# Output projection in row-split runs behind the first layer, one sum moved from GpSimd to VectorE, and the last product cut in two

## The chip, the core and the metric

The kernel runs on one core of a Trainium2 chip. The time is device time in microseconds, the median of several executions. The record gives each execution a state, fast or slow, by its time and its granted TensorE clock (1.0 is full speed). Engines are named as the profile names them: PE is TensorE, DVE is VectorE, ACT is ScalarE, POOL is GpSimd, SP is the engine that issues transfers.

## The reference

One transformer block on x of 2048 rows and 576 columns: linear attention with 32 heads of width 18, then a feed-forward layer of width 4608. Only its second half matters here:

```python
x = x + ga * _A_ref(h, A_wqkv, A_w_phi, A_wo)      # attention, ends in "o @ wo"
h = _layernorm(x, axis=-1) * (1 + cb) + sb
x = x + gb * _B_ref(h, B_w1, B_w2)                 # relu(h @ w1) @ w2
```

## The kernel before

After a first part (weights, keys, values, queries; some 93 us) the kernel goes through eight blocks of two row tiles (256 rows). Each block has a first layer `l1` and a second layer `l2`. The second layer is done as one level of a Strassen-like scheme: seven products (`prod`) of 18 matmuls, on sums of quarter matrices, in banks X = 6, Y = 4, Z = 7 of PSUM, the memory that matmuls write. The results pass through a buffer `yt`, which has one half for each half of the output's columns. A row-split run is one in which two matmuls of 64 rows each work side by side, on the lower and the upper 64 partitions. In the gaps of block b the two tiles of block b + 1 are prepared through hooks: query sums (`q_fin`), attention numerators and their division (`num_mm`, `num_o`), a transposing transfer (`turn_dma`), the output projection (`wo_mm`), the second normalization, and the scaling of the transposed result h2 that the next first layer reads.

```python
    def wo_mm(t, pr, add_x):
        for k in range(2):
            # (add_x: first part of the kernel only)
            for ci in range(NC):                      # NC = 5 chunks of 128 rows; 576 = 4 * 128 + 64
                pe.matmul(pr[:, k, 0:HD], lhsT=oT[:, t % 2, ci, :], rhs=wo_sb[:, ci, k * HD:(k + 1) * HD],
                          start=(ci == 0 and not add_x), stop=(ci == NC - 1))

    def l1_rest(js, u, hb):                           # the row-split run: two halves of 64 rows side by side
        for n, j in enumerate(js):
            for hf in range(2):
                b0 = 64 * hf
                pe.matmul(PS[:, 2 * u + hf, n * 256:n * 256 + 256], lhsT=w1b[b0:b0 + 64, j * P:(j + 1) * P],
                          rhs=hb[b0:b0 + 64, 4, :], start=False, stop=False, skip_group_check=True)

    # l1: three groups g; in each: full chunks, l1_rest for u = 0..2, remaining full chunks and relu, hooks(g, u)
    # l2: seven prod; hooks(pos) ahead of every nine matmuls
        prod(Y, A12, B21, al, True)
        fin(t, 0, Y, 0)
        if b > 0:
            pool.tensor_tensor(out=A12, in0=A12, in1=U2, op=ALU.subtract)
    # ... A12 is read again by the last product, prod(Z, A12, B22, al)

        def in_l1(g, u):
            # ...
            if (g, u) in ((0, -1), (0, 1)):
                # q_fin(q), q_in(q + NL)
            if (g, u) in ((1, 2), (2, 1)):
                t = t0 + g - 1
                pr = pair(3)                          # banks 6 and 7
                num_mm(t, pr)
                num_o(t, pr)
                turn_dma(oT[:, t % 2], o_sb[:, t % 2, :])

        def in_l2(pos):
            # pos 1 and 4: wo_mm, residual addition, statistics; pos 2 and 6: normalization, turn_dma to h2;
            # pos 12: five tensor_scalar that scale h2
```

The softmax here doesn't subtract the row's maximum and nothing guards it: scores larger than these inputs give would overflow.

## Time and profile before

| | before |
|---|---|
| time | 392.11 us (391.75 to 392.55, the 3 runs known before the change ran) |
| span of the profiled execution | 390.7 us |
| first part, until the first matmul of block 0 | 93.5 us |
| each of blocks 0 to 6, first matmul to first matmul | 37.05 us |
| block 7, first matmul to last matmul's start | 33.63 us |
| from there to the end | 4.20 us |

### The profile page before, as it was taken

What the parts mean: (1) busy time and instruction counts of PE and PEld (TensorE: products, weight loads), DVE (VectorE), ACT (ScalarE), POOL (GpSimd) and SP (SyncE); (2) the same over time, 40 slices, a digit from 0 to 9 for tenths busy, and PEclk for the clock granted to TensorE, in tenths of its full rate; (3) what the DMA queues carried; (4) which work ended last, traced back from release to release, by engine and by line L of the source; (5) the groups of instructions that cost most, each with busy time, mean ns of one, the idle gap of its engine ahead of it and who ended that gap; (6) DMA issues with size and microseconds to landing.
All of it is one profiled execution on the core that took longest, in us unless ns stands there. A gap on an engine that the chain in (4) does not pass through costs nothing.

```text
span 390.7 us, 8908 instructions
## 1 busy us (share of the span) xinstructions
PE 383.8 (98%) x3693; PEld 311.7 (80%) x3693; DVE 244.3 (63%) x452; ACT 157.9 (40%) x360; POOL 142.3 (36%) x199
## 2 busy tenths in 40 slices
PE   8999999999999999999999999999999999999995
PEld 4778888878887888788888878887888788878874
DVE  0889998854879746573755567458555664653221
ACT  1798779699531233124213510531143123312510
POOL 2155858741101510740164045306510641072045
PEclk9999999999999999999999999999999999999999
DMA  7999739795732151125313311450143124010001
GB/s 291 418 420 403 274 133 354 178 306 161 189 65 35 47 121 20 35 61 109 35 27 83 80 35 32 107 65 19 47 93 35 24 69 51 18 34 33 3 0 32
DMA packets 49515, 44.36 MB, mean 114 GB/s; under 512 B 39361, under 2 KB 42050, under 8 KB 48706
## 3 DMA queue, kind: packets, MB, share of 16 engines
q1 hardware_dynamic: 49186, 43.59, 39.6%
q8 instruction: 29, 0.48, 0.5%
q10 hardware_dynamic: 288, 0.19, 0.2%
q14 instruction: 12, 0.10, 0.1%
HBM read 27.97 MB, written 6.49 MB: 88 GB/s over the span
## 4 chain that ended last, share of the span: by engine, by line
PE 86%; POOL 6%; ACT 2%; DVE 2%; DMA 2%; issue 1%; SPq 0%; POOLq 0%; DVEq 0%; ACTq 0%
PE PS L683 33%; PE PS L742 29%; PE PS L274 9%; PE PS L410 5%; PE PS L690 5%; POOL wo_sb L637 2%; PE PS L235 2%; PE PS L391 1%; ACT RT L279 1%; POOL RH L754 1%; DMA gatd<-gt 1%; PE PS L324 1%; POOL RT L291 1%; DMA ga_row<-gatd 1%; DVE st L240 1%
## 5 line engine op out<-in xcount | busy, mean ns | idle before, releaser
L683 PE MATMUL PS<-h,R 128*128 128x256 bf16 x1152 | 133.5, 273 | 0.0
L683 PEld LDWEIGHTS <-R 128*128 128x128 bf16 x1152 | 109.8, 98 | 17.5 <-issue 5.1
L742 PEld LDWEIGHTS <-RH 128*128 128x128 f16 x864 | 84.5, 98 | 21.8
L728 POOL TENSOR_TENSOR yt<-yt,gb_row 128x288 f32<-128x288 f32 x23 | 16.8, 731 | 167.0 <-DVE yt L727 167.0
L742 PE MATMUL PS<-R,RH 128*128 128x288 bf16 (+1 forms) x576 | 75.6, 286 | 0.0
L697 ACT ACTIVATE RH<-PS 128x256 f16<-128x256 f32 x72 | 27.7, 384 | 114.0 <-PE PS L690 107.4
L699 DVE SCALAR_TENSOR_TENSOR RH<-PS,RH 128x256 f16<-128x256 f32 x72 | 30.1, 419 | 68.2 <-ACT RH L697 68.2
L279 ACT ACTIVATE RT<-PS,rs 128x576 bf16<-128x576 f32 x64 | 43.0, 750 | 7.5 <-PE PS L274 7.1
L698 ACT ACTIVATE RH<-PS 128x512 f16<-128x512 f32 x72 | 42.9, 595 | 7.8 <-PE PS L683 6.5
L746 ACT ACTIVATE RS<-PS 128x288 f32<-128x288 f32 x24 | 9.9, 411 | 75.9 <-PE PS L742 75.9
L742 PE MATMUL PS<-RT,RH 128*128 128x288 f16 x288 | 37.9, 286 | 0.0
L274 PE MATMUL PS<-RH,R 116*128 116x288 bf16 x240 | 31.8, 286 | 0.5 <-ACT RH L631 0.5
L754 POOL TENSOR_TENSOR RH<-RH,RT 128x2304 f16<-128x2304 f16 x7 | 31.8, 4548 | 0.0
L274 PE MATMUL PS<-RH,RT 116*128 116x288 bf16 x240 | 31.7, 286 | 0.0
L274 PEld LDWEIGHTS <-R 116*128 116x128 bf16 x240 | 22.9, 98 | 6.4 <-issue 0.7
L274 PEld LDWEIGHTS <-RT 116*128 116x128 bf16 x240 | 22.7, 98 | 5.5
L420 DVE TENSOR_SCALAR xn<-x_sb,mv,rs 128x576 bf16<-128x576 bf16 (+1 forms) x28 | 22.4, 842 | 7.3 <-ACT rs L415 7.3
L729 POOL TENSOR_TENSOR x_sb<-yt,x_sb 128x288 bf16<-128x288 f32 x31 | 22.8, 737 | 5.9 <-DVE yt L725 4.1
L240 DVE BATCH_NORM_STATS2 st<-x_sb 128x6 f32<-128x288 bf16 x60 | 24.2, 445 | 0.5
L410 PE MATMUL PS<-wo_sb,oT 128*128 128x288 bf16 x160 | 22.6, 286 | 0.2 <-POOL wo_sb L637 0.2
L284 DVE TENSOR_REDUCE Rk<-RT 128x64 f32<-128x1152 bf16 x16 | 21.2, 1332 | 1.4 <-ACT RT L279 1.4
L284 DVE TENSOR_REDUCE Rq<-RT 128x64 f32<-128x1152 bf16 x16 | 21.5, 1342 | 0.0
(115 smaller groups left out, 414.2 us busy)
## 6 DMA issues: line engine op xcount, KB each, us to landing
R<-in_w1a_dram SPq DMA_DIRECT2D x4, 1152.0 KB
eqd<-RT SPq DMA_DIRECT2D x14, 288.0 KB, 5.8
RT<-eqd SPq DMA_DIRECT2D x14, 288.0 KB, 2.7
R<-in_w2a_dram SPq DMA_DIRECT2D x3, 864.0 KB, 10.4
R<-in_w2b_dram SPq DMA_DIRECT2D x2, 1296.0 KB, 10.9
out_dram<-x_sb SPq DMA_DIRECT2D x15, 144.0 KB, 3.3
RT<-in_xT_dram SPq DMA_DIRECT2D x2, 640.0 KB
x_sb<-in_xk_dram SPq DMA_DIRECT2D x3, 288.0 KB
```

The costliest lines, as they stand in the source:

```text
L240: dve.bn_stats(out=s[:, hf, :], in_=x_sb[:, t, hf * HD:(hf + 1) * HD])
L274: pe.matmul(pr[:, k, 0:HD], lhsT=xt(t, ck), rhs=w[0:R, ck, k * HD:(k + 1) * HD], start=(ck == 0), stop=(ck == NC - 1))
L279: act.activation(out=E.rearrange("p (b h s e) -> p b h s e", b=2, s=2, e=DH)[:, :, :, s, :], in_=pr[:, :, 0:HD].rearrange("p b (h e) -> p ...
L284: dve.tensor_reduce(out=Rr, in_=E.rearrange("p (c e) -> p c e", e=DH), axis=AXX, op=ALU.add)
L410: pe.matmul(pr[:, k, 0:HD], lhsT=oT[:, t % 2, ci, :], rhs=wo_sb[:, ci, k * HD:(k + 1) * HD], start=(ci == 0 and not add_x), stop=(ci == NC ...
L683: pe.matmul(PS[:, 2 * u + hf, n * 256:n * 256 + 256], lhsT=w1a[:, ci, jj * P:(jj + 1) * P], rhs=hb[:, ci, :], start=(n == 0 and ci == 0), ...
L697: act.activation(out=A11[:, j, :], in_=lo[:, :, 0, :], func=ACT.Relu)
L698: act.activation(out=A2[:, j, :, :], in_=PS[:, 2 * u + 1, :].rearrange("p (n s f) -> p n s f", n=2, s=2), func=ACT.Relu)
L699: dve.scalar_tensor_tensor(out=U3[:, j, :], in0=lo[:, :, 1, :], scalar=0.0, in1=A11[:, j, :], op0=ALU.max, op1=ALU.subtract)
L729: pool.tensor_tensor(out=x_sb[:, t, c], in0=y, in1=x_sb[:, t, c], op=ALU.add)
L742: pe.matmul(PS[:, bank, 0:HD], lhsT=am[:, j, :], rhs=bm[:, j, :], start=first and j == 0, stop=(j % 9 == 8), skip_group_check=True)
L754: pool.tensor_tensor(out=A12, in0=A12, in1=U2, op=ALU.subtract)
```

## The change

Its intent: the projection's fifth chunk has only 64 real rows, and still costs two full matmuls a tile. From block 2 on, these 64 rows lie twice (in both halves of the partitions), so that both column halves run as one row-split pair, right behind the first layer's own row-split run. For that, attention moves forward in the block, and the query sums into the block before. One 2304-wide sum goes from GpSimd to VectorE from block 2 on. The last product of the kernel is cut into two column halves.

```diff
+    def wo_rest(t, pr):
+        for k in range(2):
+            b0 = 64 * k
+            pe.matmul(pr[:, k, 0:HD], lhsT=oT[b0:b0 + 64, t % 2, 4, :], rhs=wo_sb[b0:b0 + 64, 4, k * HD:(k + 1) * HD],
+                      start=True, stop=False, skip_group_check=True)
+    # wo_full: the chunks 0 to 3, eight full matmuls
         if b > 0:
-            pool.tensor_tensor(out=A12, in0=A12, in1=U2, op=ALU.subtract)
+            (pool if b == 1 else dve).tensor_tensor(out=A12, in0=A12, in1=U2, op=ALU.subtract)
 # in l1, after the l1_rest of a group:
+            hooks(g, "rest")
 # hooks of the first layer
+            if b < 2:
+                # as before, and:
+                if b and (g, u) == (2, 2):
+                    q_next(t0 + 2)
+                return
+            if (g, u) in ((0, 0), (0, 2)):
+                attend(t0 + u // 2)
+            if g and u == "rest":
+                wo_rest(t0 + g - 1, pair(3))
+            if g and u == 0:
+                t = t0 + g - 1
+                wo_full(t, pair(3))
+                add_res(t, pair(3))
+                bn(1, t)
+            if (g, u) == (1, 2):
+                norm2(b, t0)
 # hooks of the second layer: norm2 of the second tile at pos 1, scaling of h2 at pos 8 (pos 12 if b < 2)
+            if b > 1 and pos in (4, 10) or b == 1 and pos == 8:
+                q_next(t0 + 2 + pos // 8)
 # attend: before its turn_dma
+        if t > 5:
+            act.activation(out=o_sb[:, t % 2, D:640], in_=o_sb[:, t % 2, 512:D], func=ACT.Copy)
 # tail of the last block: yl = part of the result, made ready on VectorE and GpSimd ahead of fin(t + 1, 0, X, None)
+        for i, bank in enumerate((Z, 0)):
+            c, g = slice(i * H4, (i + 1) * H4), slice(HD + i * H4, HD + (i + 1) * H4)
+            for j in al:
+                pe.matmul(PS[:, bank, c], lhsT=A12[:, j, :], rhs=B22[:, j, c], ...)
+            dve.tensor_tensor(out=yt[:, 0, c], in0=PS[:, bank, c], in1=gb_row[:, g], op=ALU.mult)
+            dve.tensor_tensor(out=x_sb[:, t, g], in0=yt[:, 0, c], in1=yl[:, c], op=ALU.add)
 # layout of the input wo
+    wo[D:] = g["A_wo"][512:]
```

(The lines with # are remarks.)

More of the change, by code (lines that the diff above doesn't have):

```diff
@@ L403, in turn_dma, with wo_mm @@
         sp.dma_start_transpose(dst, src.rearrange("p (c f) -> p c f", f=P))
-    def wo_mm(t, pr, add_x):
+    def wo_mm(t, pr, add_x=False):
         for k in range(2):
@@ L411, in wo_mm, with add_res @@
                           start=(ci == 0 and not add_x), stop=(ci == NC - 1))
+    def add_res(t, pr):
+        x = v2(x_sb[:, t, :])
+        dve.tensor_tensor(out=x, in0=x, in1=pr[:, :, 0:HD], op=ALU.add)
     def ln2_rs(t):
@@ L415, in ln2_rs, with ln2_apply @@
         act.activation(out=rs2[:, t, 0:1], in_=lnv[:, t:t + 1], func=ACT.Exp, scale=-0.5)
-    def ln2_apply(t, src):
+    def ln2_apply(t, src=None):
         def cols(o, i):
@@ L466, in tile_block @@
     SS = RS[:, 0:6 * HD].bitcast(FP32).rearrange("p (a f) -> p a f", f=HD)
+    yl = RE[:, 0:2 * HD].bitcast(FP32)
     X, Y, Z = 6, 4, 7
@@ L763, in l2 @@
         fin(t + 1, 1, Z, 2)
+        H4 = HD // 2
+        if b + 1 == NB:
+            dve.tensor_tensor(out=yl[:, H4:HD], in0=PS[:, Z, H4:HD], in1=SS[:, 1, H4:HD], op=ALU.add)
+            dve.tensor_copy(out=yl[:, 0:H4], in_=SS[:, 1, 0:H4])
+            pool.tensor_tensor(out=yl, in0=yl, in1=gb_row[:, HD:D], op=ALU.mult)
+            pool.tensor_tensor(out=yl, in0=yl, in1=x_sb[:, t, HD:D], op=ALU.add)
         prod(X, A22, T4, al)
@@ L771, in l2, with q_next, attend, wo_full @@
             return
-        rows, z = slice(t * P, (t + 1) * P), yt[:, 1, :]
+        rows = slice(t * P, (t + 1) * P)
         sp.dma_start(outf[rows, 0:HD], x_sb[:, t, 0:HD])
-        pool.tensor_tensor(out=z, in0=SS[:, 1, :], in1=gb_row[:, HD:D], op=ALU.mult)
-        pool.tensor_tensor(out=z, in0=z, in1=x_sb[:, t, HD:D], op=ALU.add)
-        prod(Z, A12, B22, al)
-        dve.tensor_tensor(out=yt[:, 0, :], in0=PS[:, Z, 0:HD], in1=gb_row[:, HD:D], op=ALU.mult)
-        dve.tensor_tensor(out=x_sb[:, t, HD:D], in0=yt[:, 0, :], in1=z, op=ALU.add)
+        for i, bank in enumerate((Z, 0)):
+            c, g = slice(i * H4, (i + 1) * H4), slice(HD + i * H4, HD + (i + 1) * H4)
+            for j in al:
+                pe.matmul(PS[:, bank, c], lhsT=A12[:, j, :], rhs=B22[:, j, c], start=(i == 1 and j == 0),
+                          stop=(j == NK - 1), skip_group_check=True)
+            dve.tensor_tensor(out=yt[:, 0, c], in0=PS[:, bank, c], in1=gb_row[:, g], op=ALU.mult)
+            dve.tensor_tensor(out=x_sb[:, t, g], in0=yt[:, 0, c], in1=yl[:, c], op=ALU.add)
         sp.dma_start(outf[rows, HD:D], x_sb[:, t, HD:D])
     NB = NT // 2
+    def q_next(q):
+        if q < NT:
+            q_fin(q)
+            if q + NL < NT:
+                q_in(q + NL)
+    def attend(t):
+        pr = pair(3)
+        num_mm(t, pr)
+        num_o(t, pr)
+        if t > 5:
+            act.activation(out=o_sb[:, t % 2, D:640], in_=o_sb[:, t % 2, 512:D], func=ACT.Copy)
+        turn_dma(oT[:, t % 2], o_sb[:, t % 2, :])
+    def wo_rest(t, pr):
[3 more added lines that the diff above has]
+                      start=True, stop=False, skip_group_check=True)
+    def wo_full(t, pr):
+        for k in range(2):
+            for ci in range(4):
+                pe.matmul(pr[:, k, 0:HD], lhsT=oT[:, t % 2, ci, :], rhs=wo_sb[:, ci, k * HD:(k + 1) * HD],
+                          start=False, stop=(ci == 3), skip_group_check=True)
+    def norm2(b, t):
+        ln2_rs(t)
+        ln2_apply(t)
+        i = t % 2
+        turn_dma(h2[:, (b + 1) % 2, :, i * P:(i + 1) * P], xn[:, i, :])
     for b in range(NB):
@@ L788, in in_l1 @@
                 return
-            if (g, u) in ((0, -1), (0, 1)):
-                q = t0 + max(u, 0)
-                q_fin(q)
-                if q + NL < NT:
-                    q_in(q + NL)
-            if (g, u) in ((1, 2), (2, 1)):
-                t = t0 + g - 1
-                pr = pair(3)
-                num_mm(t, pr)
-                num_o(t, pr)
-                turn_dma(oT[:, t % 2], o_sb[:, t % 2, :])
+            if b < 2:
+                if (g, u) in ((0, -1), (0, 1)):
+                    q_next(t0 + max(u, 0))
+                if (g, u) in ((1, 2), (2, 1)):
+                    attend(t0 + g - 1)
+                if b and (g, u) == (2, 2):
[6 more added lines that the diff above has]
+            if g and u == 0:
+                t = t0 + g - 1
+                wo_full(t, pair(3))
[3 more added lines that the diff above has]
+                norm2(b, t0)
         def in_l2(pos):
@@ L803, in in_l2 @@
                 return
-            if pos in (1, 4):
+            if b < 2 and pos in (1, 4):
                 i = pos // 4
-                t = t0 + i
-                pr = pair(i)
-                wo_mm(t, pr, False)
-                dve.tensor_tensor(out=v2(x_sb[:, t, :]), in0=v2(x_sb[:, t, :]), in1=pr[:, :, 0:HD], op=ALU.add)
-                bn(1, t)
-            if pos in (2, 6):
-                i = pos // 4
-                t = t0 + i
-                ln2_rs(t)
-                ln2_apply(t, None)
-                turn_dma(h2[:, (b + 1) % 2, :, i * P:(i + 1) * P], xn[:, t % 2, :])
-            if pos == 12:
+                wo_mm(t0 + i, pair(i))
+                add_res(t0 + i, pair(i))
+                bn(1, t0 + i)
+            if b < 2 and pos == 2:
+                norm2(b, t0)
+            if pos == (6 if b < 2 else 1):
+                norm2(b, t0 + 1)
+            if pos == (12 if b < 2 else 8):
                 hb = h2[:, (b + 1) % 2]
```

## The prediction

> **What bounds the kernel now.** I read the page first: span, busy shares, clock.
>
> ```profile
> span 390.7 us, 8908 instructions
> ...
> PE 383.8 (98%) x3693; PEld 311.7 (80%) x3693; DVE 244.3 (63%) x452; ACT 157.9 (40%) x360; POOL 142.3 (36%) x199
> ...
> PEclk9999999999999999999999999999999999999999
> ```
>
> TensorE is busy 98% of the span at the full granted clock, and no other engine passes 63%. Busy shares can hide waits, so the next view is the chain of work that ended last, in order of time, for one steady block (block 5, 278.93 to 315.98 us). Columns: start, duration, what.
>
> ```profile
> 278.93 3.06 PE PS L683 x28
> 281.99 0.76 PE PS L690 x12
> 282.75 5.35 PE PS L683 x48
> ...
> 296.32 0.38 PE PS L391 x10
> 296.69 1.31 PE PS L683 x12
> 298.00 1.20 PE PS L742 x9
> 299.20 1.23 PE PS L410 x10
> 300.43 3.31 PE PS L742 x27
> 303.73 1.23 PE PS L410 x10
> 304.96 11.03 PE PS L742 x90
> ```
>
> The whole block is TensorE and the pieces join end to end: 37.05 us, the period of all seven blocks that prepare a next one. Rates: L683 (full, 256 wide) 3.06/28 = 0.109 us each; L742 and L410 (full, 288 wide) 11.03/90 = 0.1226 us each; L690 (64 rows, 256 wide) 12 in 0.76. The output projection is the two L410 runs, 2.46 us a block. Two things are not at the plain rate. Six pairs of L690 at 0.109 would be 0.66 us, so its run costs some 0.1 us more. And the first nine L742 take 1.20 instead of 9 x 0.1226 = 1.10 us. For that I looked at the timeline around 298 us.
>
> ```profile
> 296.16 0.54 PE L391 MATMUL PS<-kvz,RE 128*128 128x76 bf16 x10
> ...
> 297.12 0.76 DVE L399 TENSOR_TENSOR o_sb<-PS,rden 128x576 bf16<-128x576 f32 x1
> ...
> 297.94 1.26 PE L742 MATMUL PS<-R,RH 128*128 128x288 bf16 x9
> ```
>
> L391 (attention numerators) writes banks 6 and 7; VectorE's L399 reads them until 297.88; 0.06 us later the first product starts, which overwrites bank 6. TensorE waited about 0.1 us for VectorE here. In the chain 1.19 or 1.20 stands at this place in each of the seven blocks; the last block, without attention, goes through at the plain rate (36 in 4.42).
>
> Last, the timeline of the tail.
>
> ```profile
> 382.51 0.46 DVE L727 TENSOR_TENSOR yt<-PS,RS 128x288 f32<-128x288 f32 x1 [6.16 <-POOL RH L754]
> 383.05 0.73 POOL L728 TENSOR_TENSOR yt<-yt,gb_row 128x288 f32<-128x288 f32 x1 [0.57 <-DVE yt L727]
> ...
> 384.42 2.37 PE L742 MATMUL PS<-R,RH 128*128 128x288 bf16 x18
> ...
> 385.98 0.33 SPq L766 DMA_DIRECT2D out_dram<-x_sb  x1
> ...
> 386.89 0.46 DVE L777 TENSOR_TENSOR yt<-PS,gb_row 128x288 f32<-128x288 f32 x1 [1.75 <-PE PS L742]
> 387.49 0.46 DVE L778 TENSOR_TENSOR x_sb<-yt 128x288 bf16<-128x288 f32 x1
> 387.98 0.33 SPq L779 DMA_DIRECT2D out_dram<-x_sb  x1
> ```
>
> The chain names GpSimd's 4.5 us sum (L754) here, but I do not read it as the bound: the product that L727 needs ended at the same moment (the next 18 start at 384.42 - 18 x 0.1226 = 382.21; their predecessor is readable about 0.3 us later). The end hangs on TensorE, two VectorE operations and one store.
>
> **What the Trainium skill says.** "TensorEngine Tiling (Array Packing)", Key Properties: changing the tiling mode drains the TensorE, while tiles of one mode work in parallel. The trace agrees: a row-split run costs 0.1 us over its six pair times. "TensorE: Matmul & The Clock Gate", Back-to-back issue gap: N/2.4 + 2.5 ns, 122.5 for N = 288 (measured 122.6) and 62.5 for N = 144 (no such full matmul here; taken as an estimate). "SBUF — State Buffer", Who interferes with whom: a VectorE operation in a two-port mode and a GpSimd operation exclude each other. It agrees: the normalization (L420) beside L754 took 2.89 us, elsewhere in the block 0.64. "VectorE: DVE Perf Modes", the errata section: an fp32 tensor_tensor takes (N+151)/0.96 ns, 457 for 288 (measured 0.46 us), so 307 for 144.
>
> **Part 1, the projection (blocks 2 to 6, ten tiles).** Ten full matmuls a tile become eight, plus two of 64 rows. The fifth chunk has only 64 real rows; their copy at partitions 64 to 127 lets both column halves run as one pair, in banks 6 and 7, directly behind the L690 run, so no mode change is added. Before: 10 x 0.1226 = 1.226. After: 8 x 0.1226 + one pair 0.123 = 1.104. Gain 0.122 a tile, 1.22 us in ten.
>
> **Part 2, the wait at the products.** Attention moves to the first group of the first layer, and the last reader of banks 6 and 7 becomes the residual addition (0.75 us) behind the third group's first part; 20 matmuls (2.2 us) follow before the product. The 0.095 us wait should go: 5 x 0.095 = 0.48 us. Blocks 0 and 1 keep the old order.
>
> **Part 3, work moved off TensorE.** L754 (4.55 us on GpSimd) becomes about 1.36 us on VectorE, the duration of the same sum in block 0. Its reader is the last product of the block, 13 us after the first or later: no gain for TensorE in itself. VectorE's second-layer stretch gains this 1.36 and two query sums (1.34 + 0.35 each), and loses two residual additions, their statistics and one normalization to the first layer. It was busy 11.9 of 18 us; there is room. ScalarE gets ten copies of 64 columns, some 0.3 us each.
>
> **Part 4, the tail.** The last product is split in two halves of 144 columns: 36 x 62.5 = 2.25 instead of 18 x 122.5 = 2.21 us, +0.04. The last two VectorE operations shrink from 0.46 to 0.31 each. Against that stands a reuse. The half products go through the same half of yt that GpSimd's addition for the next row tile still reads, and two GpSimd operations now come ahead of that addition: from 383.05 five at 0.81, 0.69, 0.81, 0.69, 0.73 end at 386.8 instead of 385.96. Only then can the first half start: 386.84, then two pairs with spacings of about 0.45 and 0.23 (scaled from 0.60 and 0.38 between the long ones), last end 388.3 instead of 387.95. The tail loses about 0.35. The store before it (144 KB, 3.3 us to landing) also starts 0.85 later and lands together with the last one, so I take +0.4.
>
> **Sum.** -1.22 - 0.48 + 0.4 = -1.3 us: 392.1 - 1.3 = 390.8.
>
> **Rivals.** (a) A wait takes the place of the one removed: the pair needs the transposed output. The numerators now start at the block's start + 3.75 and the pair is due at + 10.6. Numerators 0.38, reciprocal and product on VectorE 1.3, ScalarE's copy 0.3, transpose 2.6 to landing: ready near + 8.7, nearly 2 us early. The slowest transpose took 4.3, which still just fits. For a stall: ScalarE takes its work in order, so the copy holds back the second relu until VectorE is done. If it stalled 0.5 us in each of five blocks, the gain would be gone: about 393. (b) VectorE becomes the bound at the seam between blocks (in block 5, its scaling of h2 before 315.98 is already close). In blocks 2 to 6 that scaling comes earlier now, but block 1 has two query sums more. One late seam costs 1 us: about 392. (c) The tail gains after all, if GpSimd's addition is early enough or the stores overlap better: -0.25 instead of +0.4, so 390.1. (d) GpSimd's relief is worth more, if the chain through L754 were real: then up to 1 us in the last block, 389.8. Against it stands the coincidence at 382.5 with the product's own end.
>
> **Range and chances.** The projection's gain is counted from exact rates and nearly certain; the wait's is likely; the tail is uncertain by half a microsecond either way, and a small new wait is the main danger upward. Range 390.0 to 391.8. Two per cent is 7.8 us; the projection as a whole is 2.46 us a block, and nothing here could save or cost that much: 0.98 within, 0.01 on either side.
>
> **What would show it.** Right: the chain is still all TensorE with blocks 2 to 6 near 36.7 us and blocks 0 and 1 at 37.05; the row runs with the pair last 0.88 instead of 0.76; the full part of the projection is 8 in 0.98; the first nine products take 1.10; L420 no longer has 2.9 us cases from block 2 on; in the tail the first half operation on VectorE starts when GpSimd's last addition ends. Wrong: TensorE waits ahead of the 64-row pair or at a block's first matmuls, a block at 37 us or more, or a last store issued no later, relative to the last matmul, than before.

## The result

The changed kernel takes 390.91 us (390.52 to 391.73, 4 runs); the kernel before took 392.23 us (391.75 to 392.55, 4 runs). The ratio is 0.9969, with a 95% interval of 0.9954 to 0.9984: within 2%, and clear of 1. Ratios here and below are taken from the fast runs of the same rounds; they are not quite the ratio of the medians that are quoted.

The page of the changed kernel, first its head, engine shares and clock:

```profile
span 389.3 us, 8937 instructions
...
PE 381.7 (98%) x3711; PEld 310.7 (80%) x3711; DVE 244.6 (63%) x462; ACT 157.6 (40%) x370; POOL 119.6 (31%) x193
...
PEclk9999999999999999999999999999999999999998
```

TensorE is still the bound. GpSimd lost 22.7 us of work, VectorE's total hardly moved. The chain of work of block 5, in order of time (start, duration, what):

```profile
277.83 3.06 PE PS L688 x28
280.89 0.76 PE PS L695 x12
281.65 0.48 PE PS L391 x10
...
287.75 0.76 PE PS L695 x12
288.51 0.12 PE PS L815 x2
288.63 1.09 PE PS L821 x8
289.71 5.24 PE PS L688 x48
...
299.11 15.43 PE PS L748 x126
```

L688, L695 and L748 are the old L683, L690 and L742. The projection is L815 (the pair of 64 rows, 0.12 us) and L821 (eight full matmuls). All 126 matmuls of the seven products now go at one rate, 15.43/126 = 0.1225 us, with no slow start. The change out of the row-split mode was charged to the L683 run behind it before (5.35 us for 48); now L821 carries it (1.09 instead of 8 x 0.1225 = 0.98), and the 48 of L688 take 5.24.

Where the time went, from the start times of the matmuls:

| us | before | changed | changed, once more |
|---|---|---|---|
| first part | 93.52 | 92.83 | 92.37 |
| blocks 0 and 1, each | 37.05 | 37.05 | 37.05 |
| block 2 | 37.05 | 37.31 | 37.31 |
| blocks 3 to 6, each | 37.05 | 36.71 | 36.71 |
| block 7 to its last matmul | 33.63 | 33.74 | 33.74 |
| from there to the end | 4.20 | 4.44 | 4.45 |

So four blocks gain 0.34 us each, block 2 loses 0.26 where it should have gained 0.34, and the tail loses. (The right column is a later run of the unedited changed kernel.) The 0.6 us of block 2 are a new wait, which the timeline of the changed kernel shows at the seam of blocks 1 and 2:

```profile
157.14 4.54 POOL L760 TENSOR_TENSOR RH<-RH,RT 128x2304 f16<-128x2304 f16 x1
...
159.17 2.89 DVE L424 TENSOR_SCALAR xn<-x_sb,mv,rs 128x576 bf16<-128x576 bf16 x2 [1.21 <-ACT rs L419]
...
163.78 0.25 POOL L346 TENSOR_TENSOR ratq<-Rq,rq 128x32 f32<-128x32 f32 x1 [2.10 <-DVE rq L343]
...
165.37 2.69 DVE L872 TENSOR_SCALAR h<-h,mod 128x256 bf16<-128x256 bf16 x5
...
166.04 1.42 POOL L735 TENSOR_TENSOR x_sb<-yt,x_sb 128x288 bf16<-128x288 f32 x2
...
167.60 2.60 PE L688 MATMUL PS<-h,R 128*128 128x256 bf16 x21 [0.29 <-DVE h L872]
```

Block 2 starts at 166.93 with two matmuls, and the third waits until 167.60 for L872, VectorE's scaling of h2, whose five operations take 2.69 us instead of 1.78. They stop while GpSimd's additions (L735) run, until 167.46. The third matmul comes 0.45 us late and the fourth another 0.15. The same place before:

```profile
166.06 1.78 DVE L820 TENSOR_SCALAR h<-h,mod 128x256 bf16<-128x256 bf16 x5
166.22 0.77 POOL L729 TENSOR_TENSOR x_sb<-yt,x_sb 128x288 bf16<-128x288 f32 x1 [0.64 <-DVE yt L725]
...
167.62 1.58 PE L683 MATMUL PS<-h,R 128*128 128x256 bf16 x13
```

There only one addition of GpSimd fell beside the scaling, and it started after the scaling had. In the changed kernel, GpSimd's queue in block 1 is late. The 4.5 us sum (L760) stayed there in this block, but it stood there before too, without such a wait. New is the query sum behind it: its VectorE part follows the normalization (L424, 2.89 us beside the sum), its GpSimd part (L346) waits for that, and the additions come after it, so that three GpSimd operations instead of one now fall beside the scaling.

The tail of the changed kernel:

```profile
384.27 0.74 POOL L735 TENSOR_TENSOR x_sb<-yt,x_sb 128x288 bf16<-128x288 f32 x1
...
385.04 0.31 DVE L791 TENSOR_TENSOR yt<-PS,gb_row 128x144 f32<-128x144 f32 x1 [1.67 <-POOL x_sb L735]
...
386.28 0.33 SPq L793 DMA_DIRECT2D out_dram<-x_sb  x1
```

The first half operation L791 starts just as GpSimd's addition for the other tile ends (384.27 + 0.74 = 385.01).

### The profile page after: what moved, and what is told of

Read it like the earlier page. It is cut to its first block, busy times and chain, and to the rows that moved or that the text cites. A ratio compares the mean times of both kernels' runs of the same rounds, so it can differ in the third digit from the quotient of the medians.

```text
span 389.3 us, 8937 instructions
## 1 busy us (share of the span) xinstructions
PE 381.7 (98%) x3711; PEld 310.7 (80%) x3711; DVE 244.6 (63%) x462; ACT 157.6 (40%) x370; POOL 119.6 (31%) x193
## 4 chain that ended last, share of the span: by engine, by line
PE 87%; DVE 4%; DMA 3%; ACT 2%; POOL 2%; issue 1%; SPq 1%; POOLq 0%; DVEq 0%; ACTq 0%
PE PS L688 33%; PE PS L748 30%; PE PS L274 9%; PE PS L695 5%; PE PS L821 3%; PE PS L410 2%; PE PS L391 2%; DMA R<-in_wsc_dram 1%; ACT RT L279 1%; PE PS L324 1%; DVE RT L479 1%; DMA gatd<-gt 1%; DVE st L240 1%; DMA ga_row<-gatd 1%; PE PS L251 1%
## 5 line engine op out<-in xcount | busy, mean ns | idle before, releaser
L688 PE MATMUL PS<-h,R 128*128 128x256 bf16 x1152 | 132.8, 273 | 0.3 <-DVE h L872 0.3
L688 PEld LDWEIGHTS <-R 128*128 128x128 bf16 x1152 | 111.1, 98 | 15.5 <-issue 2.5
L748 PEld LDWEIGHTS <-RH 128*128 128x128 f16 x846 | 82.8, 98 | 20.8
L734 POOL TENSOR_TENSOR yt<-yt,gb_row 128x288 f32<-128x288 f32 x23 | 23.1, 1002 | 192.1 <-DVE yt L733 192.1
L748 PE MATMUL PS<-R,RH 128*128 128x288 bf16 (+1 forms) x558 | 72.4, 286 | 0.0
L704 DVE SCALAR_TENSOR_TENSOR RH<-PS,RH 128x256 f16<-128x256 f32 x72 | 29.0, 414 | 65.6 <-ACT RH L702 65.6
L748 PE MATMUL PS<-RT,RH 128*128 128x288 f16 x288 | 37.9, 286 | 0.0
L274 PEld LDWEIGHTS <-RT 116*128 116x128 bf16 x240 | 22.7, 98 | 5.5
L733 DVE TENSOR_TENSOR yt<-PS,RS 128x288 f32<-128x288 f32 x23 | 10.4, 453 | 26.2 <-PE PS L748 19.2
L735 POOL TENSOR_TENSOR x_sb<-yt,x_sb 128x288 bf16<-128x288 f32 x31 | 22.6, 730 | 2.4 <-DVE yt L731 0.6
L695 PE MATMUL PS<-h,R 64*128 64x256 bf16 x288 | 19.9, 271 | 0.0
L291 POOL TENSOR_TENSOR RT<-RT,ratq 128x576 bf16<-128x576 bf16 x16 | 19.0, 1190 | 1.2
```

The source lines that it names most:

```text
L274: pe.matmul(pr[:, k, 0:HD], lhsT=xt(t, ck), rhs=w[0:R, ck, k * HD:(k + 1) * HD], start=(ck == 0), stop=(ck == NC - 1))
L688: pe.matmul(PS[:, 2 * u + hf, n * 256:n * 256 + 256], lhsT=w1a[:, ci, jj * P:(jj + 1) * P], rhs=hb[:, ci, :], start=(n == 0 and ci == 0), ...
L704: dve.scalar_tensor_tensor(out=U3[:, j, :], in0=lo[:, :, 1, :], scalar=0.0, in1=A11[:, j, :], op0=ALU.max, op1=ALU.subtract)
L734: pool.tensor_tensor(out=y, in0=y, in1=gb_row[:, c], op=ALU.mult)
L735: pool.tensor_tensor(out=x_sb[:, t, c], in0=y, in1=x_sb[:, t, c], op=ALU.add)
L748: pe.matmul(PS[:, bank, 0:HD], lhsT=am[:, j, :], rhs=bm[:, j, :], start=first and j == 0, stop=(j % 9 == 8), skip_group_check=True)
```

## The experiments

All kernels gave correct results. The theory after the result: a tile gains 0.122 us by the pair and a block 0.095 us by the removed wait; the seam of block 2 loses 0.6 us to GpSimd's late work in block 1; the tail loses up to 0.35 us; the first part's 0.7 us are chance. The rival: GpSimd's relief, or the moved place, brings the gain.

**The sum on VectorE in block 1 too**

```diff
-            (pool if b == 1 else dve).tensor_tensor(out=A12, in0=A12, in1=U2, op=ALU.subtract)
+            dve.tensor_tensor(out=A12, in0=A12, in1=U2, op=ALU.subtract)
```

> The changed kernel, with the 2304-wide sum on VectorE in block 1 too. The changed kernel's trace has block 2 at 37.31 us against 36.71 for blocks 3 to 6: after its second matmul TensorE waits some 0.6 us for VectorE's scaling of h2. Theory: that scaling was late because in block 1 GpSimd holds the 4.5 us sum, and then everything behind it, beside VectorE's scaling. With the sum on VectorE, block 2 takes 36.71 us and the kernel is 0.6 us shorter than the changed one (about 390.3 us); all other blocks stay. Rival: VectorE simply has too much to do in block 1 (two query sums were added); then another 1.36 us on it leaves the wait or makes it longer, block 2 at 37.3 to 38.5 us.

Measured: 390.50 us, ratio to before 0.9960 (0.9944 to 0.9977). Block 2 takes 36.72 us, and the other blocks are as they were. Timeline of this run at the seam:

```profile
165.51 1.78 DVE L872 TENSOR_SCALAR h<-h,mod 128x256 bf16<-128x256 bf16 x5
...
167.07 3.11 PE L688 MATMUL PS<-h,R 128*128 128x256 bf16 x27
```

The scaling is back at 1.78 us, and block 2 starts with 27 matmuls in a row. VectorE had one more 1.36 us operation and was still in time, so it was not too much work but GpSimd's long sum, and the queue behind it, that made the scaling late. The normalization takes 0.64 us in this run, and the query sum's GpSimd part comes 2.2 us earlier in the block. The theory holds.

**The sum on GpSimd in all blocks**

```diff
-            (pool if b == 1 else dve).tensor_tensor(out=A12, in0=A12, in1=U2, op=ALU.subtract)
+            pool.tensor_tensor(out=A12, in0=A12, in1=U2, op=ALU.subtract)
```

> The changed kernel, with the sum on GpSimd in all blocks from 1 on, as before the change. Theory: the reader of the sum comes so much later that the engine does not matter for TensorE: blocks 3 to 6 stay at 36.71 us, block 2 at 37.3, tail within 0.1 us, whole time within 0.2 us of the changed kernel (391). Rival: GpSimd's relief is a part of the gain; then blocks 3 to 6 grow to 36.9 us or more, or TensorE waits at their first matmuls as in block 2 (37.3).

Measured: 393.64 us, ratio 1.0039 (1.0024 to 1.0054): longer than before, within 2% but clear of 1. Blocks 2 to 6 take 37.68, 37.54, 37.54, 37.08 and 36.72 us. The theory's part on the sum falls. Timeline of this run in the second layer of block 2:

```profile
195.17 6.44 DVE L872 TENSOR_SCALAR h<-h,mod 128x256 bf16<-128x256 bf16 x5
195.18 4.64 POOL L760 TENSOR_TENSOR RH<-RH,RT 128x2304 f16<-128x2304 f16 x1
...
201.53 0.45 DVE L733 TENSOR_TENSOR yt<-PS,RS 128x288 f32<-128x288 f32 x1
...
202.03 2.37 PE L748 MATMUL PS<-R,RH 128*128 128x288 bf16 x18 [0.20 <-DVE yt L733]
```

The scaling of h2, which the new order puts earlier, now falls beside GpSimd's sum and takes 6.44 us. The next VectorE operation, L733, reads bank 7, and the last product must not add to that bank before; it starts 0.37 us late (488 ns after the matmul ahead of it instead of 122). VectorE's second query sum is late too, and after it the transfers. In blocks 3 and 4 the first row-split pair then waits for its transposed input: in block 3 it starts 554 ns after the matmul ahead instead of 106. So the reader of the sum was indeed not the issue; the engine that the sum sat on was, through VectorE. The sum's move is needed for the new order, though it gains nothing by its own result.

**Ten full matmuls at the new place**

```diff
     def wo_rest(t, pr):
-        # the pair of 64 rows
+        pass
     def wo_full(t, pr):
-        # eight full matmuls
+        wo_mm(t, pr)
 # and without the copy of 64 columns in attend, so that the padding rows stay zero
```

> The changed kernel, with the ten full matmuls of before (zero rows kept) at the new place, instead of one pair of 64 rows and eight full ones. Theory: each tile costs 0.122 us more, blocks 3 to 6 go from 36.71 to 36.95 us, the whole 1.2 us longer than the changed kernel (about 392.1), and the first products still start without a wait. Rival: the gain came from the moved place and the relieved engines, not from the pair; then the blocks stay within 0.1 us of 36.71.

Measured: 392.17 us, ratio 1.0003 (0.9988 to 1.0018). Blocks 3 to 6 take 36.96 us, block 2 has 37.56 with the same wait at its start. The chain of this run in block 5 has, in place of the pair and the eight:

```profile
288.89 1.33 PE PS L410 x10
```

The pair is worth 0.25 us a block, 0.124 a tile, as expected. Without it the new order gives nothing in all: by block times its removed wait is eaten up by the waits at block 2 and in the tail.

**The removed wait alone, in the kernel before**

```diff
-            if (g, u) in ((1, 2), (2, 1)):
+            if (g, u) in ((1, 2), (2, 0)):
```

> The kernel before, with one edit: the second tile's attention numerators come one step earlier in the third group (after its first pair of products instead of its second). Theory: TensorE waits 0.095 us in each of blocks 0 to 6 for VectorE's reading of banks 6 and 7; with 0.87 us more time that wait goes and each block takes 36.96 us instead of 37.05, the whole 0.67 us less than before. Rival: the 0.095 us is a cost of changing from one product to the next and stays: 37.05.

Measured: 391.13 us, ratio 0.9979 (0.9964 to 0.9994). All seven blocks take 36.96 us. The chain of this run at the first products of block 5:

```profile
296.23 1.10 PE PS L742 x9
297.33 1.23 PE PS L410 x10
```

Nine products in 1.10 us instead of 1.20. It was a wait, and one word in the kernel before takes it away in seven blocks, where the change did so in five.

**The pair at the old place, in the kernel before**

```diff
-                wo_mm(t, pr, False)
+                if b > 1:
+                    wo_rest(t, pr)
+                    wo_full(t, pr)
+                else:
+                    wo_mm(t, pr, False)
 # with the copy of 64 columns for b > 1, and the doubled rows in the layout of wo
```

> The kernel before, with the pair of 64 rows and eight full matmuls in blocks 2 to 6, but at the old place among the second layer's products, so that each pair is a row-split run of its own. Theory: each pair saves 0.122 us but its two mode changes cost about 0.1 us each, so each tile loses some 0.07 us and blocks 2 to 6 take about 37.2 us against 37.05; the whole 0.7 us longer than before. Rival: mode changes cost little for a short run, or are hidden; then the blocks shrink to 36.8 us and the place does not matter.

Measured: 393.37 us, ratio 1.0020 (0.9994 to 1.0045). Blocks 2 to 6 take 37.23 us: 0.18 more than before. The chain of this run in block 2:

```profile
187.81 0.23 PE PS L787 x2
188.04 1.09 PE PS L793 x8
```

A pair that is a run of its own takes 0.23 us instead of 0.12, and the eight full ones behind it 1.09 instead of 0.98. That is two mode changes of 0.11 us against 0.12 us saved. The times alone leave it unclear, the blocks do not. The place behind the first layer's own run is what makes the pair pay.

**The tail of the kernel before**

The edit takes the tail's lines of the diff above back and leaves the rest.

> The changed kernel with the tail of the kernel before (one product 288 wide, two long VectorE operations, the two GpSimd operations behind the addition for the next tile). Theory: the changed tail costs 0.35 us (0.11 until the last matmul, 0.24 from it to the end); with the old one the time from the last block's start to the end of the span goes from 38.2 back to 37.8 us and the kernel is 0.35 us shorter than the changed one. Rival: the changed tail saves time by its shorter last operations; then this run's is longer.

Measured: 391.00 us, ratio 0.9961 (0.9944 to 0.9977). 33.63 us to the last matmul, and 4.18 from there to the end. In the trace the expected 0.35 us are there (some 0.27 of it are the last store, which takes more or less time from run to run, as told below); in the times, 0.9961 against 0.9969 (and 0.9967 in the repeated run) is in the right direction but inside the intervals.

**The half products through the other half of yt**, on top of the sum on VectorE in block 1

```diff
-            dve.tensor_tensor(out=yt[:, 0, c], in0=PS[:, bank, c], in1=gb_row[:, g], op=ALU.mult)
-            dve.tensor_tensor(out=x_sb[:, t, g], in0=yt[:, 0, c], in1=yl[:, c], op=ALU.add)
+            dve.tensor_tensor(out=yt[:, 1, c], in0=PS[:, bank, c], in1=gb_row[:, g], op=ALU.mult)
+            dve.tensor_tensor(out=x_sb[:, t, g], in0=yt[:, 1, c], in1=yl[:, c], op=ALU.add)
```

> The changed kernel with the sum on VectorE in block 1 as well, and the last half products going through the other half of yt, which GpSimd's late addition does not read. Theory: the half products' VectorE operations waited for GpSimd's addition; now the first starts about 1 us earlier, right after its matmuls, the last store is issued 0.35 us earlier relative to the last matmul (1.1 instead of 1.45 us), and the time from the last matmul's start to the end falls from 4.44 to about 4.1. Rival: the end is set by the store of the next row tile, which is issued 0.2 us after the last matmul's start; then the end stays at 4.4.

Measured: 390.24 us, ratio 0.9945 (0.9921 to 0.9970). The last store is issued 1.10 us after the last matmul's start instead of 1.45, and the end comes 3.88 us after it. Timeline of this run, the first half operation:

```profile
383.27 0.31 DVE L791 TENSOR_TENSOR yt<-PS,gb_row 128x144 f32<-128x144 f32 x1 [0.67 <-PE PS L789]
```

It now waits for its matmuls and no longer for GpSimd: the reuse of yt was the wait. That is the 0.35 us of the store's issue. The rest of the fall to 3.88 lies in the store itself, from its issue to the end: 2.78 us here, 2.99 in the changed kernel. In this run the cut tail is better than the old one (33.74 + 3.88 = 37.62 us against 33.63 + 4.20 = 37.83), but a store can take longer: in the run with the row-split projection from block 1 on (below), which has the same tail, it took 3.06 us and the tail 33.74 + 4.17 = 37.91.

**The sum on VectorE in block 1, and the old tail**

> The changed kernel with the sum on VectorE in block 1 as well and the tail of the kernel before. If both costs (0.6 us at block 2, 0.35 us in the tail) are real and independent, this is 0.95 us shorter than the changed kernel: about 389.9 us, 2.3 us under the kernel before. If the sum on VectorE in block 1 does not help, only the tail's 0.35 us remain.

Measured: 390.25 us, ratio 0.9944 (0.9926 to 0.9961). Block 2 takes 36.72 us, the tail 33.63 + 4.18. In the trace both costs are gone at once. The time fell by 0.7 us against the changed kernel's first measurement rather than 0.95, which the spread of whole executions covers.

**All together**: the sum on VectorE in block 1, the other half of yt, and the earlier numerators in blocks 0 and 1

> Together: the changed kernel, the sum on VectorE in block 1 too, the half products through the other half of yt, and in blocks 0 and 1 the second tile's numerators one step earlier. Expected from the single runs: blocks 0 and 1 at 36.96 us, blocks 2 to 6 at 36.71, 33.74 from the last block's start to the last matmul and 3.9 from it to the end. Against the changed kernel that is 0.18 + 0.60 + 0.3 to 0.55, some 1.1 us: about 389.8 us, ratio to the kernel before 0.993 to 0.995. If the parts interfere, a block is longer than that.

Measured: 389.55 us (389.26 to 390.27, 6 runs), ratio 0.9933 (0.9918 to 0.9949). Blocks 0 and 1 take 36.96 us, 2 to 6 36.71 or 36.72, then 33.74 and 3.88. Everything adds up, and this version beats both kernels: 2.55 us under the kernel before (392.10 in these rounds) and 1.29 under the changed one (390.84 in these rounds).

**The row-split projection from block 1 on**, on top of that. In block 0, the query sums of tiles 4 and 5 go into the first layer, and blocks from 1 on use the new order.

> As the combination of all waits, and the row-split projection at the new place from block 1 on, with the query sums for block 1's tiles in the first layer of block 0. Expected if block 0 has room on VectorE for two more query sums (3.4 us): block 1 at 36.71 us instead of 36.96, 0.25 us less than the combination. If not, TensorE waits at the first matmuls of block 1 or in block 0's products, and block 0 or 1 is longer than 37.05.

Measured: 391.62 us, ratio 0.9987 (0.9973 to 1.0001). A miss: block 0 takes 38.69 us, block 1 36.82. In block 0 TensorE waits 1.1 us at the first projection for its transposed input. In the trace SP issues the first of these transposes 18.2 us into the block instead of 15.2, behind two transfers of an added query sum (that they are what holds it up is argued, not tried). It waits once more at the last product, for VectorE. Block 0 has no room for two more query sums, which fits that the change begins with block 2.

**The changed kernel once more**

> The changed kernel, unedited, once more, for two open points. Theory: the time up to the first block (93.52 us in the trace of before, 92.83 in that of the changed kernel) varies from execution to execution and is no effect of the change; it falls somewhere between 92.1 and 93.6 again, while blocks 0 and 1 are 37.05, block 2 is 37.3 and blocks 3 to 6 are 36.71 as in the first trace. The time from the last matmul's start to the end was 4.44 us in the first trace and in one run with the same tail, 4.15 and 4.19 in two others: one of these two values again, so that 0.11 us of the tail's cost (until the last matmul) is certain and the rest is not. Time against before: ratio 0.996 to 0.998. Rival: the first part is really shorter in the changed kernel and never above 93.1.

Measured: 390.84 us, ratio 0.9967 (0.9954 to 0.9981). Block times as in the first trace, to 0.01 us (the right column of the table above). The first part took 92.37 us. Over all traces it lies between 92.19 and 93.52: three traces with the old order have 93.52, 93.27 and 92.19, ten with the new one (the changed kernel's two and eight edits of it) 92.37 to 93.12, mean 92.79. The rival for this point said never above 93.1, and with one trace at 93.12 and the lowest of all in the old order, I take no effect from it, though a few tenths can't be ruled out.

## Why the prediction was right

The number came out: 390.8 us predicted, 390.91 and 390.84 measured, in the range both times. Step by step:

- **Part 1, the pair: right.** 0.122 us a tile predicted; 0.124 by the run with ten full matmuls. One sign came out otherwise: "8 in 0.98" is 1.09 us, because the change out of the row-split mode, not added but moved, now falls on these eight.
- **Part 2, the wait: right.** 0.095 us a block predicted; the kernel before with earlier numerators shows 0.09 in each of seven blocks. Together a block gains 0.34 us, as predicted (36.7 us stood in the text).
- **Part 3, work moved off TensorE: wrong in one sentence.** The step that failed is "no gain for TensorE in itself", read from the reader of the sum alone. With the sum left on GpSimd the kernel takes 2.7 us more than the changed one (0.7 points of ratio), because the sum then holds up VectorE's earlier scaling of h2. "There is room" on VectorE held. The kernel as changed pays for this too: in block 1 the sum was left on GpSimd, and the 0.6 us wait at the start of block 2 has no term in the prediction's sum.
- **Part 4, the tail: right in sum by luck.** The reuse of yt was there, and the first half operation started where the prediction had it (33.95 us after the block's start, 33.97 predicted). What failed is the scaling of 0.60 us between the last two VectorE operations. That was no spacing of VectorE's own: L778 also needs the result of GpSimd's L775, which ended 0.03 us before L778 started at 387.49:

```profile
386.73 0.73 POOL L775 TENSOR_TENSOR yt<-yt,x_sb 128x288 f32<-128x288 f32 x1
```

In the changed kernel this operand is ready early, and the half operations follow each other after 0.34 us, not 0.45. So the last addition ended only 0.09 us later relative to the block's start, not 0.35. A further 0.27 us came from the last store: from its issue to the end it took 2.72 us before and 2.99 in the changed kernel. The repeated run and the run with ten full matmuls show some 3.0 too, but two edits with the same tail showed 2.7. Why it has these two values stays open.
- **Rival (b) came true in part.** It named the seam after block 1 and 1 us; 0.6 us was measured. I had its place but not its cause: not VectorE's load, as the rival said, but GpSimd's. It was left out of the sum.
- **Rival (a)**, a late transpose, did not appear in the changed kernel. It did appear where the sum stayed on GpSimd. **Rival (c)** is false as the kernel stands; with the other half of yt it is true in two of three traces (3.88 us to the end twice, 4.17 once). **Rival (d)** is false: with the sum moved and the old tail the last block takes 33.63 + 4.18 us, against 33.63 + 4.20 before, so it gains nothing. That fits the prediction's reading that the product's own end governed there.
- **Signs of being wrong.** Three that the prediction listed did appear: TensorE waits at the first matmuls of block 2, that block takes more than 37 us (37.31), and the last store is issued no later relative to the last matmul than before (1.45 us, 1.47 before).

So the sum had one term missing. Counted by the trace the change brings 5 x 0.34 = 1.70 us, less 0.60 at the seam, less 0.06 to 0.36 in the tail (traces with the changed tail): 0.74 to 1.04 us, where the prediction counted 1.3. The measured ratio is 1.2 us (0.6 to 1.8 by its interval). The interval holds the count; the 0.2 to 0.5 us between them may be the first part's variation and are not settled. So the mechanism of the gain was right, but that the forecast hit the median to 0.1 us is luck: the missing 0.60 us at the seam did not show in the whole time.

## What to carry to other kernels

Where one engine is busy without a gap, count the change in that engine's own start-to-start times block by block; 0.1 us effects are then plain, and the time of whole executions only confirms them. Here a row-split pair paid where it joined a run that was row-split already (0.12 us a tile gained), and lost where it was a run of its own (0.09 us a tile). When work is moved in time, ask not only when its result is read, but which other engine's work it will then run beside and slow down, and at every seam between an old and a new schedule check the queues once more. Before scaling a spacing between two operations, look at what the second one waits for.

## What the Trainium skill lacked or had wrong

- "TensorEngine Tiling (Array Packing)", Key Properties, says that changing the mode drains the TensorE, but gives no size. Here a change into or out of 64-row tiles cost about 0.1 us each: 0.23 instead of 0.12 us for a lone pair, 1.09 instead of 0.98 for the eight full matmuls behind it. Two of them, 0.22 us, outweigh the 0.12 us that the pair saves.
- "SBUF — State Buffer", Who interferes with whom, was right where it was tested: in block 2 the scaling of h2 took 6.44 us beside GpSimd's 4.64 us sum, and 2.25 us in the changed kernel, where the sum is on VectorE. It works the other way too: GpSimd's multiplication L734 took 1.78 us in the six cases beside VectorE's sum and 0.73 in the others.
- "VectorE: DVE Perf Modes", the errata section: its length for fp32, which the page gives as checked at 512 and 2048 elements, held at 144 too (0.31 us measured, 307 ns by the formula).
- "TensorE: Matmul & The Clock Gate", Back-to-back issue gap, says that the formula is for an isolated matmul and under-counts at small N in a stream of weight loads and matmuls (81 ns measured at N = 128, not 56), which the prediction does not mention. Here it held in such a stream: the 36 matmuls of the cut last product, N = 144, each with a weight load, start 62 or 63 ns apart, and those with N = 288 122 or 123 ns. The cut last product had its last start 0.11 us later than the uncut one, and 35 x 62.5 - 17 x 122.5 ns = 0.105 us.
